# Attention with forget gates, then a gated feed-forward: mask and decay become rows of the score contraction, q and k reach their tiles through a staging tile and a second transfer

## The chip, the cores and the metric

The kernel runs on one core of a Trainium2 chip. The core has a matrix engine (TensorE, PE in the profile, with its weight loads as PEld), a vector engine (VectorE, DVE), an activation engine (ScalarE, ACT), a general engine (GpSimd, POOL) and a queue processor (SyncE, SP) that issues nearly all DMAs here. Each engine executes its own list of instructions strictly in order, and the engines wait for each other on semaphores. The metric is the time of one execution on the device in microseconds (us), the median of several runs.

## The reference

There are 8 batches with 8 heads each, sequences of 576 positions and 64 numbers per head. Attention has a causal mask and a decay that accumulates from a forget gate `f`. A feed-forward layer follows, with a convolution of three taps along the sequence that gates its hidden layer.

```python
scores = q @ k.T / sqrt(64)
cum    = cumsum(log(clip(f, 1e-4, 1)))
scores = where(key > query, -1e9, scores + cum[query] - cum[key])
x      = softmax(scores) @ v                 # heads side by side: [8, 576, 512]
h      = relu(x @ w_in)                      # [8, 576, 1024]
conv   = w[0]*h[s-1] + w[1]*h[s] + w[2]*h[s+1]
out    = (h * sigmoid(conv)) @ w_out         # [8, 576, 512]
```

## The kernel before

**Groups.** Attention works in 16 groups of four heads, numbered `hb` 0 to 15; two groups make one batch `b`. For each group the scores are computed with keys on the partitions and queries along the free axis, in 128-wide blocks, and only where the key block is not wholly in the future. The blocks on the diagonal (`sd`, two steps per group, line 342), the blocks below it (`so`, four steps, line 364) and the 64-wide tail block (`st`, line 322) are separate steps, each filling a PSUM tile of 1024 columns, and each is followed by an exponential on ACT (`ed`, `eo`, `et`). The product with v follows (`pv`), its normalisation on DVE (`n`, `m`), a turn to the layout of the feed-forward (`t`, `tx`), and then per batch eight steps of the first feed-forward product (`f`, line 425), of the rectifier on ACT (`r`), the convolution on DVE (`c`, `d`), the gate's function on ACT (`a`), the gating on DVE (`g`), and the second product (`o`, line 469), its copy out of PSUM (`e`) and its store (`s`).

**q and k.** A group's q and k stand in one of four tiles `qk` (`RING` = 4, so that group `hb` reuses the tile of group `hb - 4`, and its steps wait for the scores of that group, the list `old` in the code). q and k are 32-bit numbers in memory. For groups 2 to 15 a transposing DMA (`q{hb}.0` for q, `q{hb}.1` for k, line 180) reads them as pairs of 16-bit halves and writes 128 partitions of 2304 columns: the odd partitions hold the upper halves, which are the numbers in bf16, and the even partitions hold the lower halves, which are not wanted. All 128 partitions go into the contraction, so the even ones must be overwritten, with zeros but for three partitions that carry the decay: `cum` in bf16 on the side of q against -1 on the side of k, and two bf16 pieces of `cum` on the side of k against 1 on the side of q. For groups 2 to 7 this is done by DVE (`cl`, line 186, one instruction per side over 128x2304) and two small DMAs from a copy of the rows in memory (`rw`, lines 202 and 203). For groups 8 to 15 it is done by DMAs alone (`fi`, lines 194 and 196): zeros from a tensor `blank` in memory and four rows (the fourth of zeros) from `image`. Groups 0 and 1 are loaded plainly and turned by TensorE (`tp`, `cl`), since they are needed at once; in group 0 the decay is added by two further matmuls per score matmul (lines 315 and 317).

**The causal mask.** In groups 0 to 7 (`MASK_PE`) a matmul ahead of each half of a diagonal step, and ahead of the tail step, writes -1e30 above the diagonal (line 320), and the scores accumulate on it. In groups 8 to 15 the exponential writes to a 32-bit tile, and POOL selects from it with an affine condition (`md`, `mt`, lines 356 and 335).

**What sets the order.** A list written out by hand (`ORDER`) names every step once. The program walks through it and appends each step's instructions to its engine's list, so the order of the names decides the order on every engine, SP's queue included; a step that has a choice of engines carries it after an `@`. Buffers go round in the order of the list. SP waits in place: a DMA whose semaphore has not arrived holds back all DMAs behind it. Every DMA also waits for the landing of the eighth before it, since eight semaphores go round.

## Time and profile before

| | |
|---|---|
| runs | 246.43, 249.28, 249.78 us; median 249.28 us |
| span of the profiled execution, from its first to its last instruction | 244.1 us |
| median of the runs less that span (launch and end lie around it) | 5.2 us |
| busy share of the span: PE, DVE, ACT, POOL | 93%, 84%, 85%, 22% |
| share of the chain that ended last on PE | 78% |
| DMA | 49.68 MB in 120176 packets, mean 204 GB/s |

A line of the profile names the engine, the line of the program, the operation, and out<-in by the names of the tiles (without buffer numbers), with shapes as partitions x elements. `SPq` is SP's queue; the duration there is the time that the issue of the DMA took, not the transfer. "Landing" is the time from the issue until the last of the transfer's semaphore updates.

### The profile page before, as it was taken

How to read it: one execution, taken by the hardware profiler on the slowest of the kernel's cores; microseconds unless marked ns; L12 is line 12 of the kernel's file. 1: busy time of each engine (PE TensorE's matmuls, PEld its weight loads, DVE VectorE, ACT ScalarE, POOL GpSimd, SP SyncE). 2: the span in 40 equal slices, each digit the busy share in tenths (PEclk: the TensorE clock that was granted, in tenths of full speed). 3: DMA queues.
4: the chain of work that ended last, by engine and by line, in shares of the span. 5: the costliest groups of instructions: out<-in, count | busy, mean ns of one | idle time of the engine just before them, and what ended most of it. 6: DMA issues, size and time to landing. Idle time of an engine off the chain costs nothing.

```text
span 244.1 us, 6385 instructions
## 1 busy us (share of the span) xinstructions
PE 226.9 (93%) x2627; PEld 145.0 (59%) x2627; DVE 205.1 (84%) x323; ACT 206.9 (85%) x278; POOL 52.9 (22%) x77
## 2 busy tenths in 40 slices
PE   0899899779999999999999999999999999999991
PEld 0787585547556676575557755675666566444440
DVE  5735359999998999999999889996998889999931
ACT  2868677999998999999999999999988995798442
POOL 8020520205220020030402570245311311000000
PEclk9999999999999999999999999999999999999999
DMA  6999999999999999999999999969999950641326
GB/s 192 328 159 243 304 204 192 202 253 279 204 188 205 228 158 240 229 314 186 198 256 246 187 209 257 273 134 222 194 260 188 236 140 3 168 157 62 142 86 216
DMA packets 120176, 49.68 MB, mean 204 GB/s; under 512 B 109759, under 2 KB 110271, under 8 KB 120147
## 3 DMA queue, kind: packets, MB, share of 16 engines
q1 hardware_dynamic: 119981, 48.97, 92.4%
q8 instruction: 20, 0.33, 0.6%
q10 hardware_dynamic: 166, 0.31, 0.4%
q14 instruction: 9, 0.07, 0.1%
HBM read 21.11 MB, written 10.17 MB: 128 GB/s over the span
## 4 chain that ended last, share of the span: by engine, by line
PE 78%; DVE 7%; DMA 6%; ACT 4%; issue 1%; ACTq 1%; SPq 1%; DVEq 0%
PE ps L474 24%; PE ps L429 20%; PE ps L312 15%; PE ps L389 7%; DMA qk<-in_q_dram 3%; PE ps L320 3%; PE ps L394 3%; PE ps L166 2%; PE ps L414 2%; DVE u L446 2%; ACT pp L370 2%; DMA pd<-in_moe_conv_w_dram 2%; DVE u L448 2%; DVE qk L186 1%; DMA qk<-image 1%
## 5 line engine op out<-in xcount | busy, mean ns | idle before, releaser
L429 PE MATMUL ps<-xt,w_in_f 128*128 128x512 f16 (+1 forms) x512 | 69.9, 286 | 0.0
L370 ACT ACTIVATE pp<-ps 128x1024 f16<-128x1024 f32 x64 | 64.7, 1032 | 4.2 <-PE ps L312 2.7
L474 PE MATMUL ps<-w_out_f,hg 128*128 128x512 f16 x288 | 66.8, 379 | 0.0
L312 PE MATMUL ps<-qk 128*128 128x128 bf16 (+2 forms) x576 | 63.4, 240 | 1.6 <-ACT pp L353 0.8
L446 DVE SCALAR_TENSOR_TENSOR u<-ht,cwt 128x576 f32<-128x576 f16 x64 | 52.7, 837 | 3.6 <-ACT ht L440 3.4
L451 ACT ACTIVATE hg<-u,cw 128x576 f16<-128x576 f32 x64 | 48.7, 782 | 5.9 <-DVE u L448 5.8
L448 DVE SCALAR_TENSOR_TENSOR u<-ht,cwt,u 128x576 f32<-128x576 f16 x64 | 53.2, 846 | 0.5
L429 PEld LDWEIGHTS <-w_in_f 128*128 128x128 f16 x512 | 34.3, 98 | 28.5
L312 PEld LDWEIGHTS <-qk 128*128 128x128 bf16 x576 | 39.2, 98 | 19.8 <-issue 3.3
L440 ACT ACTIVATE ht<-ps 128x576 f16<-128x576 f32 x64 | 41.0, 663 | 6.0 <-DVE hg L458 2.7
L474 PEld LDWEIGHTS <-hg 128*128 128x128 f16 x288 | 26.9, 98 | 28.8
L458 DVE SCALAR_TENSOR_TENSOR hg<-hg,ht 128x576 f16<-128x576 f16 x51 | 38.7, 771 | 0.6 <-ACT hg L451 0.5
L356 POOL TENSOR_SCALAR_AFFINE_SELECT pp<-pd 128x1024 f16<-128x1024 f32 x16 | 19.7, 1244 | 53.6 <-ACT pd L353 53.6
L389 PE MATMUL ps<-va,pp 128*128 128x65 f16 x640 | 24.8, 193 | 1.1 <-DVE va L217 1.0
L389 PEld LDWEIGHTS <-pp 128*128 128x128 f16 x640 | 22.6, 97 | 3.7 <-DVE va L217 1.3
L405 DVE TENSOR_TENSOR xm<-ps,rc 128x896 f16<-128x896 f32 (+1 forms) x32 | 23.9, 751 | 0.5
L353 ACT ACTIVATE pp<-ps 128x1024 f16<-128x1024 f32 x16 | 16.6, 1039 | 4.7 <-PE ps L312 3.9
L353 ACT ACTIVATE pd<-ps 128x1024 f32<-128x1024 f32 x16 | 16.2, 1023 | 1.2 <-PE ps L312 1.0
L217 POOL CAST va<-vf 128x1024 f16<-128x1024 f32 x8 | 10.0, 1252 | 32.1 <-DMA vf<-in_v_dram 27.8
L320 PE MATMUL ps<-mask,ident 128*128 128x512 bf16 (+1 forms) x40 | 14.3, 359 | 1.5 <-ACT pp L370 0.8
L403 DVE RECIPROCAL rc<-ps 128x14 f32<-128x14 f32 (+1 forms) x32 | 6.7, 208 | 8.6 <-PE ps L394 5.5
L479 ACT COPY ob<-ps 128x1024 f32<-128x1024 f32 (+1 forms) x14 | 12.9, 919 | 0.3 <-issue 0.2
(83 smaller groups left out, 176.4 us busy)
## 6 DMA issues: line engine op xcount, KB each, us to landing
vf<-in_v_dram SPq DMA_DIRECT2D x32, 256.0 KB, 7.7
out_dram<-ob SPq DMA_DIRECT2D x14, 512.0 KB, 3.7
qk<-blank SPq DMA_DIRECT2D x8, 540.0 KB, 6.2
ob<-in_moe_w_in_dram SPq DMA_DIRECT2D x4, 512.0 KB, 6.3
ob<-in_moe_w_out_dram SPq DMA_DIRECT2D x4, 512.0 KB
out_dram<-ob SPq DMA_DIRECT2D x6, 256.0 KB, 7.2
vf<-in_v_dram SPq DMA_DIRECT2D x8, 128.0 KB, 5.9
hg<-in_q_dram SPq DMA_DIRECT2D x2, 288.0 KB
```

The lines of the kernel that those rows point to most:

```text
L312: nc.tensor.matmul(o, tk[:, h * S + k0:h * S + k0 + 128], tq[:, h * S + q0:h * S + q0 + n], start=first, stop=last and not by_matmul(hb, h))
L353: nc.scalar.activation(o, ps_of(f"sd{i}").rearrange("p (s c) -> p s c", s=2), AF.Exp, scale=SCALE)
L370: nc.scalar.activation(pair(i)[:, s, 512:1536], ps_of(f"so{i}.{s}"), AF.Exp, scale=SCALE)
L389: nc.tensor.matmul(ps[:, c:c + D + 1], block(hb, h, m, n), va[:, h, m, 0:D + 1], start=(m == 0), stop=(m == n))
L405: nc.vector.tensor_tensor(xm[:, CUT * D * u:CUT * D * u + nj * k * D].rearrange("p (j x d) -> p j x d", x=k, d=D), got[:, :, :, 0:D], r.un ...
L429: nc.tensor.matmul(ps[:, t0:t1], w_in_f16[:, cc, 128 * ff:128 * (ff + 1)], xt[:, cc // 2, x:x + t1 - t0], start=(cc == 0), stop=(cc == NCC ...
L440: nc.scalar.activation(ht_of(b, ff)[:, 2:2 + S], ps_of(f"f{b}.{ff}")[:, 0:S], AF.Relu, scale=1.0 if (b, ff) in LATE else 0.5)
L446: nc.vector.scalar_tensor_tensor(u, ht[:, 1:1 + S], cwt[:, ff, 0:1], ht[:, 2:2 + S], op0=ALU.mult, op1=ALU.add)
L448: nc.vector.scalar_tensor_tensor(u, ht[:, 3:3 + S], cwt[:, ff, 1:2], u, op0=ALU.mult, op1=ALU.add)
L451: nc.scalar.activation(hg_of(b, ff), u_t[slot[f"c{b}.{ff}", "u"]], AF.Sigmoid if (b, ff) in LATE else AF.Tanh, scale=cw[:, ff, 1:2])
L458: nc.vector.scalar_tensor_tensor(hv, hv, 1.0, ht_of(b, ff)[:, 2:2 + S], op0=ALU.add, op1=ALU.mult)
L474: nc.tensor.matmul(ps[:, 512 * (c % 2):512 * (c % 2 + 1)], w, w_out_f16[:, ff, :], start=(ff == 0), stop=(ff == NFF - 1))
```

## The change

**Mask and decay as rows.** Below the 64 numbers of a head, the contraction gets further rows: four for the decay (partitions 64 to 67, two pieces of `cum` on either side) and 43 for the causal mask (68 to 110). Ordinary blocks contract over 68 rows (`ROWS`), blocks on the diagonal over 111 (`EDGE`). The mask rows hold powers of a small step on the side of q and large negative numbers on the side of k, so that a sum over the rows is near zero at and below the diagonal and hugely negative above it; each row covers three columns. POOL makes the pattern `edge` once, with one memset and eleven affine selections of 128x128, and it is then copied into partitions 64 to 127 of the four `qk` tiles, both sides (`px{t}.{side}`, eight steps of two copies over 64x2048 and 64x256): tile 0 on DVE, tiles 1 to 3 on POOL. The copies stay valid for the whole run, apart from the decay rows, which `rw` overwrites for each group. The mask matmuls, POOL's selections, DVE's `cl` of groups 2 to 7, and the tensor `blank` with its fills go away.

**Staging and a second transfer.** For groups 2 to 15 the transposing DMA now writes one of two staging tiles `sg` (`NSG` = 2), and a second DMA (`cp{hb}.{side}`, 64 partitions of 2304 bf16, 288 KB) copies its odd partitions to partitions 0 to 63 of the `qk` tile. The transposing load waits for a free `sg` tile, which means for the landing of the `cp` that read it last; `cp` waits for the landing of its load and for the scores of group `hb - 4`. `rw` is now two DMAs of two rows each for every group, and waits for the `px` steps of its tile.

**Order.** The list is the old one with the new steps put in, and the loads moved back behind the `cp` that frees their staging tile where two tiles would not do. In SP's queue around groups 8 and 9 the old program has the following (`qk1` is the tile of group 9, `qk0` that of group 8; `vf0` is the v of batch 4, `ob` are stores):

```order
L180 DMA_TRANSPOSE qk1_86<-in_k_dram 128x2304
L180 DMA_TRANSPOSE qk0_85<-in_k_dram 128x2304
L180 DMA_TRANSPOSE qk1_86<-in_q_dram 128x2304
L180 DMA_TRANSPOSE qk0_85<-in_q_dram 128x2304
L194 DMA qk1_86<-blank_66 60x4x1152
L196 DMA qk1_86<-image_65 4x2x2304
L194 DMA qk0_85<-blank_66 60x4x1152
L196 DMA qk0_85<-image_65 4x2x2304
L209 DMA vf0_89<-in_v_dram 128x8x64
```

The new program has at the same place (lines 171, 178 and 189/190 are the load, `cp` and `rw`):

```order
L171 DMA_TRANSPOSE sg0_86<-in_k_dram 128x2304
L171 DMA_TRANSPOSE sg1_87<-in_k_dram 128x2304
L178 DMA qk1_83<-sg0_86 64x2304
L171 DMA_TRANSPOSE sg0_86<-in_q_dram 128x2304
L178 DMA qk1_83<-sg0_86 64x2304
L171 DMA_TRANSPOSE sg0_86<-in_q_dram 128x2304
L189 DMA qk1_83<-image_65 2x2304
L190 DMA qk1_83<-image_65 2x2304
L178 DMA qk0_82<-sg0_86 64x2304
L178 DMA qk0_82<-sg1_87 64x2304
L189 DMA qk0_82<-image_65 2x2304
L190 DMA qk0_82<-image_65 2x2304
```

Four loads that stood in a row are now the first two in a row, and then copy, load, copy, load, and two copies, all through the tile `sg0` but for the last.

On POOL, after the memsets at the start, the old program casts v and the weights of the feed-forward as they land (`va1` is the v of group 1, without which `pv1.0` can't start):

```order
L217 CAST va0_91<-vf0_89 128x4x4x64
L219 CAST va0_91<-vf0_89 64x4x64
L518 CAST w_in_f16_69<-ob0_125 128x2x512
L217 CAST va1_92<-vf0_89 128x4x4x64
L518 CAST w_in_f16_69<-ob1_126 128x2x512
```

The new one has the copies of the pattern ahead of them (lines 183 and 185; 204 and 206 are the casts of v, 471 that of the weights; each pair of rows stands for one `px` step, and the next three pairs, for `qk2` and `qk3`, are left out at the dots):

```order
L204 CAST va0_90<-vf0_88 128x4x4x64
L206 CAST va0_90<-vf0_88 64x4x64
L183 COPY qk1_83<-edge_74 64x4x512
L185 COPY qk1_83<-edge_74 64x4x64
L183 COPY qk1_83<-edge_74 64x4x512
L185 COPY qk1_83<-edge_74 64x4x64
...
L183 COPY qk3_85<-edge_74 64x4x512
L185 COPY qk3_85<-edge_74 64x4x64
L471 CAST w_in_f16_68<-ob0_121 128x2x512
L204 CAST va1_91<-vf0_88 128x4x4x64
```

Twelve copies now stand between the cast for group 0 and the cast for group 1.

The diff, without the lines of the list but for its head, and without those declarations that only go away:

```diff
 ORDER = """
-dca cw ld0 ld1 ld0.0.0 tp0.0.0 dcl ...
+dca cw px0.0@DVE px0.1@DVE ld0 ld1 ld0.0.0 tp0.0.0 dcl ...
 """
...
+    NSG = 2
-    NCL = 8
-    MASK_PE = (0, 1, 2, 3, 4, 5, 6, 7,)
+    ROWS, EDGE = 68, 111
+    STEP, FAR = 2.0 ** -55, -2.0 ** 16
...
+    sg_t = [cpool.tile([128, HS], BF16, name=f"sg{t}") for t in range(NSG)]
...
     def turn_qk(hb, p, side):
-            nc.tensor.transpose(o[:, 128 * j:128 * (j + 1)], i[:, 128 * j:128 * (j + 1)], ident_b)
+            nc.tensor.transpose(o[0:64, 128 * j:128 * (j + 1)], i[:, 128 * j + 1:128 * (j + 1):2], ident_b)
...
-    def load_qk(hb, h0, nh, side):
+    def load_qk(hb, side):
+        src = (q, k)[side]
         nc.sync.dma_start_transpose(
-            t.bitcast(U16)[:, h0 * S:(h0 + nh) * S],
+            sg_t[slot[f"q{hb}.{side}", "sg"]].bitcast(U16),
...
-    def clamp(hb, h0, nh, side):
-    def fill(hb):
...
+    def pack(hb, side):
+        t = sg_t[slot[f"q{hb}.{side}", "sg"]]
+        odd = bass.AP(tensor=t.tensor, offset=int(t.offset) + HS, ap=[[2 * HS, 64], [1, HS]])
+        nc.sync.dma_start(qk_t[hb % RING][0:64, HS * side:HS * (side + 1)], odd)
+
+    def edge_rows(t, side, e):
+        copy = {"ACT": nc.scalar.copy, "POOL": nc.gpsimd.tensor_copy, "DVE": nc.vector.tensor_copy}[e]
+        o = qk_t[t][64:128, HS * side:HS * (side + 1)].rearrange("p (h s) -> p h s", h=HH)
+        copy(o[:, :, 0:512].rearrange("p h (m j) -> p h m j", j=128),
+             edge[64:128, side].unsqueeze(1).unsqueeze(1).broadcast_to((64, HH, 4, 128)))
+        copy(o[:, :, 512:S], edge[64:128, side, 0:SL].unsqueeze(1).broadcast_to((64, HH, SL)))
 
     def rows_of(hb):
+        c, t = slice(hb * HH, (hb + 1) * HH), qk_t[hb % RING]
+        nc.sync.dma_start(t[64:66, 0:HS], image[:, c, :].rearrange("j h s -> j (h s)"))
+        nc.sync.dma_start(t[66:68, HS:2 * HS], image[:, c, :].rearrange("j h s -> j (h s)"))
...
-    def scores(o, hb, h, k0, q0, n, m=128, first=True, last=True):
+    def scores(o, hb, h, k0, q0, n, m=128, rows=ROWS):
         tq, tk = stq_t[hb % RING], stk_t[hb % RING]
-        nc.tensor.matmul(o, tk[:, h * S + k0:h * S + k0 + 128], tq[:, h * S + q0:h * S + q0 + n],
-                         start=first, stop=last and not by_matmul(hb, h))
+        nc.tensor.matmul(o, tk[0:rows, h * S + k0:h * S + k0 + m], tq[0:rows, h * S + q0:h * S + q0 + n],
+                         start=True, stop=not by_matmul(hb, h))
...
-    def masked(o, n, j):
-    def tail_mask(hb):
-    def diag_mask(i):
...
             for side in range(2):
-                add(f"q{hb}.{side}", "SP", old, lambda hb=hb, side=side: load_qk(hb, 0, 4, side))
+                add(f"q{hb}.{side}", "SP", [], lambda hb=hb, side=side: load_qk(hb, side), take=["sg"])
+                add(f"cp{hb}.{side}", "SP", [f"q{hb}.{side}"] + old, lambda hb=hb, side=side: pack(hb, side),
+                    give=[("sg", f"q{hb}.{side}")])
+            add(f"rw{hb}", "SP", ["ki"] + old + px, lambda hb=hb: rows_of(hb))
+            ready = [[f"rw{hb}", f"cp{hb}.0", f"cp{hb}.1"]] * 2
+        ready = [r + px for r in ready]
```

More of the change, by code (lines that the diff above doesn't have):

```diff
@@ L277, in decay_image @@
     def decay_image(e):
-        for j, a, h in ((0, 0, 0), (1, 1, 0), (2, 1, 1)):
-            {"SP": nc.sync, "POOL": nc.gpsimd}[e].dma_start(image[j, a], kc[BH * h:BH * (h + 1)])
-    def constants():
-        nc.sync.dma_start(image[1:3, 0].rearrange("j h s -> h j s"), plus.unsqueeze(1).broadcast_to((BH, 2, S)))
-        nc.sync.dma_start(image[0, 1], minus)
-        nc.sync.dma_start(image[3].rearrange("a h s -> h a s"), zero.rearrange("h (a s) -> h a s", a=2))
-        nc.sync.dma_start(blank, zero[0:60])
-    def warm_up(name):
-        for x in range(2):
-            nc.tensor.matmul(ps_of(name)[:, 512 * x:512 * (x + 1)], quiet[:, 0:128], quiet, start=True, stop=True)
+        for j in range(2):
+            {"SP": nc.sync, "POOL": nc.gpsimd}[e].dma_start(image[j], kc[BH * j:BH * (j + 1)])
     def conv_weights():
@@ L521 @@
     add("cwt", "DVE", ["cw"], conv_ratios, give=[("ps", "cw")])
-    for x in range(0):
-        add(f"wu{x}", "PE", [], lambda x=x: warm_up(f"wu{x}"), take=["ps"])
-        add(f"wd{x}", "PE", [], lambda: None, behind=[f"wu{x}"], give=[("ps", f"wu{x}")])
-    add("zc", "SP", [], constants)
     add("dca", "DVE", [], lambda: nc.vector.tensor_scalar(fsb, fsb, 1e-4, 1.0, op0=ALU.max, op1=ALU.min))
@@ L534 @@
             add(f"{w}c{j}", "POOL/ACT/DVE", [f"{w}{j}"], lambda e, w=w, j=j: stage_cast(w, j, e), give=[("ob", f"{w}{j}")])
+    for t in range(RING):
+        for side in range(2):
+            add(f"px{t}.{side}", "POOL/DVE/ACT", [], lambda e, t=t, side=side: edge_rows(t, side, e))
     for hb in range(NHB):
@@ L538 @@
         was = hb - RING
+        px = [f"px{hb % RING}.{side}" for side in range(2)]
         old = [f"st{was}"] + [f"sd{2 * was + y}" for y in range(2)] + [
```

149 lines of the change are left out of this document (43 added, 106 removed).

## The prediction

> **What bounds the kernel now.** I read the page's busy shares first, then its chain, then a table by stages, and last SP's queue.
>
> ```profile
> span 244.1 us, 6385 instructions
> PE 226.9 (93%) x2627; PEld 145.0 (59%) x2627; DVE 205.1 (84%) x323; ACT 206.9 (85%) x278; POOL 52.9 (22%) x77
> PE   0899899779999999999999999999999999999991
> PE 78%; DVE 7%; DMA 6%; ACT 4%; issue 1%; ACTq 1%; SPq 1%; DVEq 0%
> 40.00:60.00 20.00, 16.67 (x247) 11.51 (x246) 19.79 (x30) 19.47 (x28) 4.29 (x4) 1.00 1.11 242
> 107.00:133.00 26.00, 26.00 (x272) 15.82 (x270) 24.66 (x36) 25.48 (x36) 6.06 (x6) 1.00 1.17 231
> ```
>
> The chain runs on PE. Of the 40 slices of 6.1 us in the third row, each from the tenth to the last but one is 90% busy or more, and from 107 to 133 us PE has no gap (the columns of the last rows are the stretch, its length, then PE, PEld, DVE, ACT and POOL busy, the granted clock, the DMA share and GB/s). From 40 to 60 PE lacks 3.3 us, with DVE and ACT full. So a matmul taken away after 60 us is worth its time, as long as its inputs come. The last figures of each row warn of that: the DMA engines have work all the time. How q and k arrive stands in SP's queue; this is the turn for groups 8 and 9:
>
> ```profile
> 84.94 0.61 SPq L203 DMA_DIRECT2D qk<-image  x1
> 85.65 6.12 SPq L180 DMA_TRANSPOSE qk<-in_k_dram  x2
> 91.82 5.02 SPq L180 DMA_TRANSPOSE qk<-in_q_dram  x2
> 96.95 0.95 SPq L194 DMA_DIRECT2D qk<-blank  x1
> ...
> 100.64 0.41 SPq L209 DMA_DIRECT2D vf<-in_v_dram  x1
> 101.11 0.57 SPq L495 DMA_DIRECT2D out_dram<-ob  x1
> ...
> 102.40 2.96 SPq L495 DMA_DIRECT2D out_dram<-ob  x1
> 105.40 2.06 SPq L209 DMA_DIRECT2D vf<-in_v_dram  x2
> 107.56 4.86 SPq L180 DMA_TRANSPOSE qk<-in_q_dram  x1
> 106.54 1.03 ACT L353 ACTIVATE pd<-ps 128x1024 f32<-128x1024 f32 x1
> PE ps L312 <- DMA qk<-image: 0.4, 1, 0.4
> ```
>
> Four loads go out back to back in 11.1 us, the fills follow, then v and stores, and 21.9 us after the first load the next turn starts. The first exponential of group 9 begins 20.9 us after its first load was issued: PE's matmuls wait for q and k only 0.4 us in the whole run (last line), but there is little to spare.
>
> **What goes away.** PE loses 40 mask matmuls, and their price is the distance to the next matmul, not the listed duration:
>
> ```profile
> L320 PE MATMUL ps<-mask,ident 128*128 128x512 bf16 (+1 forms) x40 | 14.3, 359 | 1.5 <-ACT pp L370 0.8
> 43.65 0.38 PE L320 MATMUL ps<-mask,ident 128*128 128x512 bf16 x1
> 43.87 0.38 PE L312 MATMUL ps<-qk 128*128 128x128 bf16 x4
> L356 POOL TENSOR_SCALAR_AFFINE_SELECT pp<-pd 128x1024 f16<-128x1024 f32 x16 | 19.7, 1244 | 53.6 <-ACT pd L353 53.6
> L186 DVE TENSOR_SCALAR qk<-qk,lim 128x2304 uint16<-128x2304 uint16 x12 | 10.3, 874 | 2.3 <-DMA qk<-in_q_dram 2.3
> ```
>
> That is 0.22 us for 32 of them and about half for the 8 short ones, 7.9 us in all. Groups 4 to 7 fall after 58 us, where PE is full: 3.9 us are certain if inputs come in time. Groups 0 to 3 lie where ACT, DVE and DMA share the chain, so their 3.9 may stay hidden. POOL's 19.7 us of selections were beside other work (the chain has no POOL), and of DVE's 10.3 us some is on the chain before 60 us, but there the transfers are late next. Fewer contraction rows I cost at nothing: the columns streamed stay the same, and no row here shows a score matmul with fewer rows, so I bound it by none to the masks' size either way.
>
> **What POOL adds.** Six `px` steps stand between the casts for groups 0 and 1.
>
> ```profile
> 26.68 1.04 POOL L217 CAST va<-vf 128x1024 f16<-128x1024 f32 x1
> 32.22 1.16 PE L389 MATMUL ps<-va,pp 128*128 128x65 f16 x32
> 17.51 0.39 POOL L219 CAST va<-vf 64x256 f16<-64x256 f32 x1
> ```
>
> POOL's cast takes 1.04 us for 1024 elements and 0.39 for 256; a `px` step of 2048 and 256 elements is thus about 2.5 us, between 1.3 (if bf16 copies go twice as fast) and 3.2 us. POOL is free from 17.9; six steps end at 32.9, then a weight cast, then `va1.0` at 35. `pv1.0`, which ran at 32.22, waits 2 to 3 us on PE, and everything behind it on PE too. Tile 0's copies on DVE stand ahead of the decay's sum; at the 874 ns that DVE took for 2304 columns they cost some 2 us, which the turning of group 0 hides up to 11.8 us; at half that rate group 0 starts 2 us later.
>
> **What SP adds.** The chain load, landing, `cp`, landing, next load replaces loads back to back. Its prices:
>
> ```profile
> DMA to landing us min/median/max: 4.8/6.2/6.4
> image<-kc SPq DMA_DIRECT2D x3, 72.0 KB, 3.4
> out_dram<-ob SPq DMA_DIRECT2D x14, 512.0 KB, 3.7
> qk<-blank SPq DMA_DIRECT2D x8, 540.0 KB, 6.2
> ```
>
> A load (the first row; it is that of the transfers into `qk`) lands 4.8 to 6.4 us after issue; the chain leaves less ahead of it in the queue, so I take 4.8. `cp`, from SBUF, 288 KB, has no row; 72 KB out of SBUF took 3.4, 512 KB 3.7, a fill of 540 KB behind loads 6.2. I take 3.5, with 3.3 and 6.2 as ends. The Trainium skill ("DMA: Bandwidth & Descriptors", "Anatomy of one DMA — SWDGE (gpsimd) path") fits a fixed 2.0 us plus bytes over 436 GB/s: an estimate of 2.7 for `cp`, by which each of some nine `cp`s in series would be 0.8 shorter and the sum below 7 us less. For the two rows from SBUF the fit gives 2.2 and 3.2, where this trace has 3.4 and 3.7.
>
> Groups 8/9, from the first load: landed 4.8; `cp9.1` landed 8.3; `q9.0` 13.1; `cp9.0` 16.6; `q8.0` 21.4; two `cp` issues (0.95 as the fill's) and two row DMAs (0.61) take 3.1: 24.5; v and stores as now, 100.64 to 107.56, 6.9: 31.4. Now it is 21.9, so 9.5 us are lost.
>
> ```profile
> 125.88 0.41 SPq L209 DMA_DIRECT2D vf<-in_v_dram  x1
> 127.08 6.17 SPq L209 DMA_DIRECT2D vf<-in_v_dram  x3
> 133.35 6.78 SPq L180 DMA_TRANSPOSE qk<-in_q_dram  x2
> 156.83 1.02 ACT L353 ACTIVATE pd<-ps 128x1024 f32<-128x1024 f32 x1
> 22.24 0.30 SPq L202 DMA_DIRECT2D qk<-image  x1
> 26.00 5.64 SPq L180 DMA_TRANSPOSE qk<-in_q_dram  x1
> 37.90 2.00 SPq L209 DMA_DIRECT2D vf<-in_v_dram  x3
> 40.00 0.39 SPq L202 DMA_DIRECT2D qk<-image  x1
> 63.77 3.96 SPq L180 DMA_TRANSPOSE qk<-in_q_dram  x1
> ```
>
> Groups 10/11 start with two loads (3.1 apart, half of 6.12): 7.9, then 11.4, 16.2, 19.7, 24.5, issues 27.6, v and stores 125.88 to 133.35, 7.5: 35.1 against 25.8 now, 9.3 lost. Group 12: 4.8, 8.3, 13.1, `cp13.0` behind that load about 14.5, `q12.1` 19.3, `cp12.1` 22.8, against 23.0 now from 133.35 to the scores ahead of the exponential at 156.83: nothing more.
>
> Before group 9: `rw1` waits for POOL to 23 instead of 22.24. `q3.0`, issued at 26.00, waits for the landing of `cp2.0`, issued at 24.9 behind the weights: 28.4. Two loads and three v: 36.6; `cp3.0` landed 40.1, `q4.1` 44.9, `rw3` 45.9 instead of 40.00. One more round trip beside the weights' loads to 63.77 loses some 2, groups 6/7 (4.8, 8.3, 13.1, 14.5, 19.3, issues and v 4.6: 23.9 against 21.9 from 63.77 to 85.65) another 2: about 10 in all.
>
> Sum: 10 + 9.5 + 9.3 = 28.8. Against it, the store of 2.96 us and the v of 2.06 and 6.17 were long because the queue was full (neighbours take 0.4 to 0.6); a chain that lets the DMA engines idle gives some 3 us back in each of three such blocks, 9. Remaining: 20 us by the time group 12 starts, PE having nothing else to do in its order. The 88 us from there to the end stay as they are (groups 14 and 15 come no later than that), and the masks' 3.9 and POOL's 2 to 3 vanish in the waits. So the span is 244.1 + 20 = 264, and with the 5.2 us between span and median 269 us.
>
> Ends: in series stand three loads in each of the turns from group 8 to 12 and some four before, 13, and nine `cp`s. If a load lands 1 us sooner in a shorter queue (`cp` at 3.3 adds 2), 15 us go: 254. Load and `cp` both at 6.2 add 13 x 1.4 and 9 x 2.7, 42 us: 311.
>
> **Rivals.**
>
> *The queue keeps pace.* If the landings were so short that a turn fits into PE's 25.8 us, PE would remain the bound. Groups 8/9 need three loads and two `cp`s in series, plus 10 us of issues: it decides at 15.8 us for the five, such as 3.4 for each load and 2.8 for each `cp`. For it speaks that these landings were measured in a full queue; against it, that the smallest row of a load is 4.8. Then POOL's 2.3 stay and the masks' 3.9 to 7.9 go: 243.7 to 247.7. Chance 0.13, with 0.05 of it below 244.3.
>
> *Only the beginning is late.* The waits on `old` at a load are gone, so SP may run ahead and catch up after group 5; then POOL's 2 to 3 and `rw3`'s 6 remain, less the masks of groups 4 to 7: 252 to 256, two fifths of it still within 2%. Chance 0.13.
>
> *Congested landings.* The upper ends in half of the links or more: 285 to 311. For it speaks that v and stores still precede the loads in the queue. Chance 0.11.
>
> *Half clock after waits.* The trace shows matmuls at half rate after the 7 us in which PE waited at the start:
>
> ```profile
> 8.15 3.73 PE ps L166 x36
> 15.07 0.50 PE ps L166 x9
> ```
>
> 0.104 us each, then 0.056: 1.7 us lost in one such stretch. The forecast has five waits of several us; all but the last are followed by another wait that swallows the loss, but if each counts, 8.5 us: 278. The Trainium skill ("TensorE: Matmul & The Clock Gate", "Part 1: The HAM clock gate") says that an idle window of about 3.4 us halves the clock; the trace agrees at the start, and after 11 us no wait is long enough to show it. Chance 0.08.
>
> **The numbers.** My forecast, lateness of 7 to 36 us, has 0.55. Runs of before spread by 1.3% and about 2% can be told from no change: faster means under 244.3, slower over 254.3. Faster 0.05, from the first rival; same 0.13, its other 0.08 and 0.05 of the second; slower 0.82. The range leaves out the first rival and the upper half of the congested case, 0.19: 251 to 292 us.
>
> **What would show it.** In the changed profile: successive turns of loads for groups 8/9, 10/11 and 12/13 some 28 to 32 us apart where now 22 and 26; PE's waits listed on DMA `qk<-sg` or `qk<-image`, several us each, at groups 3, 9, 8, 11 and 12; DMA share clearly under 1 between 60 and 170 us; a POOL `px` copy near 2.1 us. Wrong would be: `cp` landing in under 3 us and PE without gaps after 60 us, then the first rival holds; or SP waiting on PE at `cp`, then the queue was ahead.

## The result, and the profile after

The changed kernel takes 321.2 us (median of 4 runs, 320.5 to 323.6), the kernel before 248.1 us on the same chip: a ratio of 1.296, 95% interval 1.287 to 1.305. The direction was forecast, the size was not: 269 us were predicted, with a range of 251 to 292. In five of the variants below (short copies alone, four tiles with short copies, the beginning alone, both with 24 extra copies) one or two of the four runs, the profiled one among them, came out over 1.5% above the fastest and are left out of the ratio, though not of the median given in us.

These are lines of the changed kernel's page: span, busy times, three rows of the 40 slices (8 us each here), the first DMA queue (packets, MB, share of the time of 16 DMA engines) and the chain by engine.

```profile
span 318.8 us, 6332 instructions
PE 249.7 (78%) x2587; PEld 159.4 (50%) x2587; DVE 195.7 (61%) x305; ACT 208.0 (65%) x278; POOL 46.0 (14%) x74
PE   1997592585879549863799759993999969999993
PEclk9998598596879958995599975998699998999998
DMA  8999787969995699938994599758979999136315
q1 hardware_dynamic: 119640, 52.11, 82.6%
DMA 38%; PE 33%; SPq 17%; ACT 4%; issue 3%; DVE 2%; POOL 2%; ACTq 0%; POOLq 0%
```

Before, the chain had 78% PE and 6% DMA; now DMA and SP's queue hold 55% of it. PE is below 90% in 20 of the 40 slices, and its clock falls to 5 and 6 tenths behind the holes. The row of the queue matters most, because the prediction never used it. The same row of the kernel before reads:

```profile
q1 hardware_dynamic: 119981, 48.97, 92.4%
```

The share is the sum of the packets' times over 16 engines: 92.4% of 244.1 us, 226 us, before; now 82.6% of 318.8, 263 us. It is no exact measure of work done, since packets that are on their way together are counted each, so that it goes over 1 where transfers crowd (1.07 on average from 20 to 195 us before), and a packet that is held up counts longer. Two things happened at once: the packets take 37 us more, and what is left of the span grew from 19 to 55 us. Before, the 19 us lay at the end: in the last 49 us the share is 0.40. Now it is 0.90 from 20 to 260 us. The waits show who stands still. First the two rows of PE's waits for q, k and their rows, then SP's own queue, where L171 is the transposing load and `qk<-sg` the packing copy:

```profile
PE ps L288 <- DMA qk<-image: 41.7, 9, 9.6
PE ps L288 <- DMA qk<-sg: 6.7, 2, 4.1
SPq L171 <- DMA qk<-sg: 54.7, 14, 7.8
```

Fourteen loads stood for 54.7 us until a copy had landed and its staging tile was free. The turn for groups 8 and 9, in SP's queue of the changed kernel (start, duration, what is issued; L178 is the copy, L189 and L190 the rows):

```profile
120.40 7.32 SPq L171 DMA_TRANSPOSE sg<-in_k_dram  x2
127.89 0.49 SPq L178 DMA_DIRECT2D qk<-sg  x1
132.47 1.96 SPq L171 DMA_TRANSPOSE sg<-in_q_dram  x1
138.11 0.47 SPq L178 DMA_DIRECT2D qk<-sg  x1
142.28 1.95 SPq L171 DMA_TRANSPOSE sg<-in_q_dram  x1
144.28 0.42 SPq L189 DMA_DIRECT2D qk<-image  x1
144.76 0.25 SPq L190 DMA_DIRECT2D qk<-image  x1
146.43 1.12 SPq L178 DMA_DIRECT2D qk<-sg  x2
147.59 0.45 SPq L189 DMA_DIRECT2D qk<-image  x1
...
148.52 0.41 SPq L196 DMA_DIRECT2D vf<-in_v_dram  x1
...
155.60 7.49 SPq L171 DMA_TRANSPOSE sg<-in_q_dram  x2
```

The turn lasts 35.2 us; it was 21.9, and 31.4 were predicted. The next starts at 155.60 instead of 107.56, so 48.0 us late, and the end is 74.7 us late.

The trace also gives the time of each DMA packet. These are the packets of 4608 bytes, which but for some 60 are the rows of the packing copies (number, median and 95th percentile in ns, their sum over 16 engines), and the sum of all packets:

```
kernel     4608-byte packets   median   95%    sum/16    all packets, sum/16
before           85             305     371     1.5 us        228.3 us
after          1852             478     721    51.1 us        266.6 us
```

A copy is 64 such packets, so 28 copies take about 50 us of all 16 engines, 1.8 us each. What went away, the fills of 2304-byte packets, freed 17.5 us (26.2 to 8.7).

### The profile page after: what moved, and what is told of

The parts are those of the page before. It is cut to its first block, busy times and chain, and to the rows that moved or that the text cites. A ratio compares the mean times of both kernels' runs of the same rounds, so it can differ in the third digit from the quotient of the medians.

```text
span 318.8 us, 6332 instructions
## 1 busy us (share of the span) xinstructions
PE 249.7 (78%) x2587; PEld 159.4 (50%) x2587; DVE 195.7 (61%) x305; ACT 208.0 (65%) x278; POOL 46.0 (14%) x74
## 3 DMA queue, kind: packets, MB, share of 16 engines
q1 hardware_dynamic: 119640, 52.11, 82.6%
## 4 chain that ended last, share of the span: by engine, by line
DMA 38%; PE 33%; SPq 17%; ACT 4%; issue 3%; DVE 2%; POOL 2%; ACTq 0%; POOLq 0%
DMA qk<-sg 20%; PE ps L427 12%; SPq L171 9%; PE ps L288 8%; PE ps L382 8%; DMA qk<-image 6%; DMA sg<-in_q_dram 5%; DMA sg<-in_k_dram 3%; SPq L196 3%; DMA vf<-in_v_dram 3%; PE ps L342 2%; DMA u<-in_f_dram 2%; SPq L189 2%; PE ps L367 1%; SPq L448 1%
## 5 line engine op out<-in xcount | busy, mean ns | idle before, releaser
L288 PE MATMUL ps<-qk 111*128 111x128 bf16 (+3 forms) x576 | 73.1, 270 | 55.9 <-DMA qk<-image 41.7
L288 PEld LDWEIGHTS <-qk 68*128 68x128 bf16 (+2 forms) x576 | 44.0, 112 | 76.9 <-issue 36.1
L382 PE MATMUL ps<-xt,w_in_f 128*128 128x512 f16 (+1 forms) x512 | 73.7, 295 | 0.1
L313 ACT ACTIVATE pp<-ps 128x1024 f16<-128x1024 f32 x32 | 32.6, 1023 | 62.8 <-PE ps L288 61.5
L427 PE MATMUL ps<-w_out_f,hg 128*128 128x512 f16 x288 | 71.2, 397 | 0.0
L323 ACT ACTIVATE pp<-ps 128x1024 f16<-128x1024 f32 x64 | 64.6, 1025 | 9.4 <-PE ps L288 7.2
L427 PEld LDWEIGHTS <-hg 128*128 128x128 f16 x288 | 27.9, 101 | 31.7 <-issue 4.4
L342 PE MATMUL ps<-va,pp 128*128 128x65 f16 x640 | 29.3, 207 | 0.8 <-ACT ht L393 0.8
L342 PEld LDWEIGHTS <-pp 128*128 128x128 f16 x640 | 27.5, 108 | 4.1 <-issue 1.2
L358 DVE TENSOR_TENSOR xm<-ps,rc 128x896 f16<-128x896 f32 (+1 forms) x32 | 23.9, 753 | 0.5
L206 POOL CAST va<-vf 64x256 f16<-64x256 f32 x6 | 5.2, 860 | 103.7 <-PE ps L288 58.9
L370 DVE COPY xt<-ps 128x1152 f16<-128x1152 f16 x9 | 6.8, 757 | 10.9 <-PE ps L367 7.9
L183 POOL COPY qk<-edge 64x2048 bf16<-64x2048 bf16 x6 | 11.4, 1908 | 0.0
```

The source lines that it names most:

```text
L288: nc.tensor.matmul(o, tk[0:rows, h * S + k0:h * S + k0 + m], tq[0:rows, h * S + q0:h * S + q0 + n], start=True, stop=not by_matmul(hb, h))
L313: nc.scalar.activation(pair(i)[:, :, 0:512], ps_of(f"sd{i}").rearrange("p (s c) -> p s c", s=2), AF.Exp, scale=SCALE)
L323: nc.scalar.activation(pair(i)[:, s, 512:1536], ps_of(f"so{i}.{s}"), AF.Exp, scale=SCALE)
L342: nc.tensor.matmul(ps[:, c:c + D + 1], block(hb, h, m, n), va[:, h, m, 0:D + 1], start=(m == 0), stop=(m == n))
L382: nc.tensor.matmul(ps[:, t0:t1], w_in_f16[:, cc, 128 * ff:128 * (ff + 1)], xt[:, cc // 2, x:x + t1 - t0], start=(cc == 0), stop=(cc == NCC ...
L427: nc.tensor.matmul(ps[:, 512 * (c % 2):512 * (c % 2 + 1)], w, w_out_f16[:, ff, :], start=(ff == 0), stop=(ff == NFF - 1))
```

## The experiments

The first theory was the prediction's own, sharpened by the wait of 54.7 us: **the serial chain**, load, copy, load, through two staging tiles in a queue that issues in order. Its rivals were the **bytes** of the copies, the **beginning** (late casts on POOL, copies behind the weights), and the **half clock** of PE.

**Four staging tiles, loads at their old places.**

```diff
-    NSG = 2
+    NSG = 4
-    RING, NP, NPT, NVA, ..., NOB = 4, 6, 4, 4, ..., 4
+    RING, NP, NPT, NVA, ..., NOB = 4, 6, 3, 3, ..., 3
-... q9.1 t5 a1.7 tx5@DVE q8.1 so12.1 ... cp9.1 q9.0 cp9.0 q8.0 rw9 sd15 ...
+... q9.1 t5 a1.7 tx5@DVE q8.1 q9.0 so12.1 ... q8.0 f2.0 cp9.0 cp9.1 rw9 sd15 ...
```

> The changed kernel with four staging tiles instead of two and with the loads of q and k, the packing copies and the row transfers at the places that loads, clamps and fills had before the change (all loads of a turn back to back, copies behind them). To make room there are three tiles of v's casts, of output stages and of tail probabilities instead of four. Theory (serial chain: a load cannot be issued before the copy that frees its staging tile has landed, and the queue of SP stands still meanwhile): the four loads of a turn go out within about 12 us again, PE's waits on q and k fall from about 60 us to under 15, the mean clock comes back to at least 0.97 from 0.868, and the time is 250 to 262 us. Rival 1 (the copies' bytes: 28 copies of 288 KB more on DMA engines that were full already): the bytes are the same, so the time stays above 300 us. Rival 2 (the late casts of POOL at the start, and the half clock that follows): the start is the same, so at least the first 30 us of lateness up to group 5 stay, 280 us or more.

Measured: 289.2 us, ratio 1.166 (1.158 to 1.174). The chain theory alone falls: no load waits for a copy any more, yet only 32 of 73 us come back. The bytes alone, which were to keep the time above 300 us, fall too; the 280 us or more of a late beginning are not contradicted. The same turn in SP's queue, the four loads, and the DMA row and queue of that run:

```profile
112.51 10.35 SPq L171 DMA_TRANSPOSE sg<-in_k_dram  x2
122.90 4.49 SPq L171 DMA_TRANSPOSE sg<-in_q_dram  x2
DMA  7998299999999999999999999999999995072315
q1 hardware_dynamic: 119640, 52.11, 96.0%
```

The loads go out back to back, but issuing them takes 14.8 us where it took 11.1, with the engines now at 90% or more in all slices but two from the second to the 33rd: 96.0% of 289.0 us is 277 us of packet time. That looks like a bound of its own; the runs with short copies test it.

**Four staging tiles, the changed order kept.** The edit is the first two pairs of lines above.

> The changed kernel with four staging tiles (and the same three smaller pools as in the run before), but the changed kernel's order of loads and copies is kept. A load then no longer waits for the copy ahead of it to land; but SP still stands at each copy until the load of that copy has landed. Theory (serial chain): of each link of about 5 us for a load and 4.2 to 5.6 us for a copy the second half goes, so about half of the 73 us comes back: 275 to 292 us, and the turn of groups 8 and 9, 35.2 us now, is 26 to 30 us. Rival 1 (bytes): above 300 us. Rival 3 (only the waiting for a free tile matters, not SP's standing at the copies): as with the old order, 250 to 262 us.

Measured: 295.4 us, ratio 1.194 (1.187 to 1.200), a little above what the chain theory gave. The turn of groups 8 and 9 takes 31.4 us, where 26 to 30 were expected. Freeing the loads from the copies brings 26 us, putting them back to back another 6. In both runs the engines are full most of the time (94.6% here), so the two are not to be read as the full worth of each half.

**Copies of an eighth of the columns, all else as changed.**

```diff
-        ... ap=[[2 * HS, 64], [1, HS]])
-        nc.sync.dma_start(qk_t[hb % RING][0:64, HS * side:HS * (side + 1)], odd)
+        n = HS if hb < RING else HS // 8
+        ... ap=[[2 * HS, 64], [1, n]])
+        nc.sync.dma_start(qk_t[hb % RING][0:64, HS * side:HS * side + n], odd)
```

> The changed kernel with its two staging tiles and its order, but from group 4 on each packing copy moves only the first 288 of the 2304 columns; the rest of the scores is made from the columns of earlier groups. Waits and queue are as before, the bytes of 24 copies fall from 6.9 MB to 0.9 MB. Theory (serial chain, in which a copy's landing is a fixed part and its bytes, 288 KB at about 150 GB/s being 1.9 us): each copy lands 1.7 us sooner, about 2.5 instead of 4.2; with about 11 copies in series from group 4 to 13 the time falls by 15 to 25 us to 296 to 306 us. Rival 1 (bytes): 6.0 of 52.8 MB are gone, so about 36 us: 280 to 287 us.

Measured: 277.2 us, ratio 1.115 (1.107 to 1.124): 44 us less with the chain left as it was, even more than the bytes' number. The packets of 4608 bytes fell from 51.1 to 7.7 us of engine time. SP's waits of loads for a copy fell from 54.7 to 30.9 us. So the bytes count, through the engines' time and through each copy's landing; this run does not divide the two.

**Both at once.**

> Both edits at once: four staging tiles with the old places of the loads, and packing copies of 288 of 2304 columns from group 4 on (the rest of the scores is made from columns of earlier groups). Apart they gave 289 and 277 us, where the whole change takes 321. Theory (two causes that add: the copies' time on the 16 DMA engines, 2.3 us of each copy, and the serial chain through two tiles that leaves the engines idle): from group 5 on the kernel runs at the pace of before, 175 us from the first exponential of group 5 to the end, which starts at about 88 to 90 us as in both single runs: 260 to 270 us with the 5 us around the span. Rival (either alone is enough, since the longer of the two sets the pace): 274 to 280 us, as with short copies alone.

Measured: 262.3 us, ratio 1.054 (1.046 to 1.063), where the theory of two adding causes had put it. From the first exponential of group 5, at 84.4 us, the kernel runs nearly at the pace of before (180.1 us to the end, against 175.4); most of what is left, 15.7 us, lies ahead of it.

**The bytes in the kernel before.** 24 extra copies, for whose data no engine waits:

```diff
+    spare = cpool.tile([64, 2304], BF16, name="spare")
+    for x in range(24):
+        add(f"xx{x}", "SP", [], lambda: nc.sync.dma_start(spare,
+            w_in_f16.rearrange("p c f -> p (c f)")[0:64, 0:2304].bitcast(BF16)))
```

> The kernel before the change with 24 extra copies of 288 KB from SBUF to a spare tile of 64 partitions (0 to 63, 4608 bytes each), spread over SP's transfers of groups 4 to 14. No instruction of another engine waits for them; three tiles of v's casts, output stages and tail probabilities instead of four make the room. This is the price of the copies' bytes alone, without chain, staging or mask rows. Theory (bytes: each copy holds the 16 DMA engines for 2.0 to 2.3 us, and these were busy for 228 of 244 us): 276 to 283 us of engine time, so 265 to 285 us. Rival (only the chain and the waits of SP cost): 248 to 254 us.

Measured: 283.0 us, ratio 1.134 (1.123 to 1.145). No staging and no mask rows, and 34 us are lost, nearly as much as the change loses with four tiles (41). But the run is not free of a chain: all 24 copies write the one tile `spare`, and SP stood at ten of them until the copy before had landed. SP's wait in this run and, below it, in the next one, with 128 partitions:

```profile
SPq L527 <- DMA spare<-w_in_f: 18.0, 10, 3.9
SPq L527 <- DMA spare<-w_in_f: 9.9, 8, 3.3
```

So the 34 us are the price of the bytes and of this standing together, and how much each of them has is not shown. PE and DMA of this run, in slices of 7.1 us:

```profile
PE   0998798797699869859995899579899499999992
DMA  7999999999999799899999999999999792073315
```

DMA is at 90% or more in all but two slices from the second to the 31st, and PE is below 90% in 17 of the first 32. The three smaller pools are part of the 34 us; the run without a full copy below has them too, and loses 9 us in all.

**The same bytes to 128 partitions**, `spare` being 128 x 1152 and the source 128 partitions too:

> As the run with 24 extra copies to 64 partitions, at the same places and with the same 288 KB each, but to 128 partitions of 2304 bytes. In the changed kernel a packet of 4608 bytes to partitions 0 to 63 takes 478 ns in the median where the first ones of a lone copy take 180, and packets of 2304 bytes to partitions spread over all 128 take 93 to 111 ns. Theory (the writes of partitions 0 to 63 share half of the ways into SBUF and hold the engines up): packets of about 100 ns, 24 copies cost 20 us of engine time instead of 50, 250 to 262 us. Rival (the bytes cost the same wherever they land): the same time as with 64 partitions.

Measured: 267.1 us, ratio 1.070 (1.060 to 1.081), 5 us above the range given but 16 us below the run with 64; 8 us less of SP's standing may be part of that. The packets:

```
extra copies          packets        median     sum/16    per copy
to partitions 0-63    24 x 64,4608 B  362 ns    34.3 us    1.43 us
to all 128            24 x 128,2304 B 100 ns    22.9 us    0.95 us
```

The sums are those of the size class less what the kernel before has in it (1.5 and 26.2 us). So a copy confined to 64 partitions takes half as much engine time again as the same bytes over 128. The Trainium skill ("SBUF — State Buffer", "Door 1: The DMA port swizzle (why `[64,N]` ≈ `[32,N]`)") says that partitions 0 to 63 reach only 8 of SBUF's 16 DMA ports and gives 196 GB/s for them, at 1 MiB, against 328 over all 128. The runs agree in direction: 1.43 to 0.95 is a factor of 1.5, the page's figures make 1.7. Source, destination and the packets' length changed together here, so which of them does it stays open.

**The beginning alone.**

```diff
-... px1.1@POOL px2.0@POOL px2.1@POOL px3.0@POOL px3.1@POOL cwt ...
+... px1.1@POOL cwt ...
-... st1 wi0 so2.0 sd3 wi2 wic0@POOL wi3 et1 eo2.0 cp2.0 cp2.1 rw2 n0.0 ... wic2@POOL ...
+... st1 px2.0@DVE px2.1@DVE cp2.0 cp2.1 rw2 wi0 so2.0 sd3 wi2 wic0@POOL wi3 et1 eo2.0 n0.0 ... wic2@POOL px3.0@POOL px3.1@POOL ...
```

> The changed kernel with only its beginning altered: the two packing copies and the rows of group 2 are issued ahead of three of the weights' transfers (1.5 MB) instead of behind them, the mask rows of ring tile 2 are copied by DVE, and those of tile 3 by POOL behind the casts of the weights. Theory (the first 15 us of lateness come from there: the copy of group 2 landed at 35 us behind the weights, and the loads of group 3 wait for it): the first exponential of group 3 comes at 48 to 53 us instead of 60.1, and the whole takes 308 to 314 us. Rival (the later chain catches the gain, since it sets its own pace from the loads of group 4 on): 318 to 322 us.

Measured: 320.3 us, ratio 1.280 (1.265 to 1.294): nearer to the rival. By the ratio it is some 318 us, 3 to 4 less than the changed kernel, with intervals that overlap. In the profiled run group 2's first exponential comes at 31.7 instead of 36.8 us, group 3's at 57.3 instead of 60.1, and by group 5 (90.4 and 91.0) nothing is left of it. There, time won ahead of the chain is lost in it.

**PE kept busy in its waits.**

```diff
+    WARM = {"sd5": 14, "sd6": 36, "sd9": 13, "sd10": 11, "sd13": 30, ...}
+    def warm(name):
+        for _ in range(WARM.get(name, 0)):
+            nc.tensor.matmul(ps_of(name)[:, 0:512], ident_b, ident_b.unsqueeze(1).broadcast_to((128, 4, 128)), ...)
     def diag_scores(i):
         ps = ps_of(f"sd{i}")
+        warm(f"sd{i}")
```

> The changed kernel with 183 extra matmuls of 512 columns on constant tiles, put on TensorE ahead of the eleven score steps at which it waited 2.2 to 9.6 us for q, k or their rows (52 us in all); they fill about four fifths of each wait (0.22 us each, 40 us in all), so that the clock is not cut. Their results are overwritten. Theory (half clock after the waits is on the path: PE was busy for 249.7 us with 40 matmuls fewer than before's 226.9): the mean granted clock comes back over 0.95 and the time falls by 10 to 20 us to 300 to 312 us. Rival (the chain of loads and copies sets its own pace and swallows what PE loses): clock back, time within 316 to 326 us.

Measured: 321.9 us, ratio 1.303 (1.293 to 1.313), with the mean clock at 0.944 instead of 0.868. Two stretches of the changed kernel, and below them the same two of this run (stretch, length, busy time of PE, PEld, DVE, ACT, POOL, granted clock, DMA share, GB/s):

```profile
50.00:60.00 10.00, 0.96 (x10) 0.99 (x11) 2.95 (x4) 1.04 (x2) 0.00 (x0) 0.70 1.14 170
120.00:155.00 35.00, 23.41 (x259) 16.08 (x256) 22.46 (x33) 20.67 (x29) 2.05 (x2) 0.79 0.88 138
```

```profile
50.00:60.00 10.00, 6.65 (x33) 2.91 (x31) 2.18 (x3) 0.27 (x1) 0.00 (x0) 0.97 1.01 158
120.00:155.00 35.00, 29.90 (x295) 17.36 (x293) 22.03 (x33) 20.00 (x29) 2.39 (x2) 0.95 0.81 133
```

The clock is back and the time is not. The extra matmuls did not swallow the gain themselves: behind them PE still waited 20.9 us for the rows of q and k, and the first exponentials of groups 9 and 12 come when they did (148.3 and 224.8 us, against 148.2 and 224.3). So the slow clock is a mark that the waits leave, not a cause of the 73 us.

**The complete change with order and beginning repaired**: four tiles, loads at their old places, and the beginning as above.

> The changed kernel, complete, with four staging tiles and the old places of the loads (289 us so far), and with the beginning altered as in the run of the beginning alone: the copies and rows of group 2 ahead of the last three transfers of w_in, the mask rows of ring tile 3 behind the casts. Theory (the copies' bytes bound it: 277 us of engine time in the run with four tiles, 96% of its span): 282 to 288 us, little gained. Rival (the 17 us of lateness at group 5 come from the beginning, and are independent of the rest): 270 to 276 us.

Measured: 281.8 us, ratio 1.138 (1.129 to 1.146), just under what the theory gave. In the run with four tiles one weight transfer had stood for a cast (three issues took 9.9 us instead of 1.4, as there were fewer output stages); that is gone here too. Its DMA row and queue:

```profile
DMA  7999999999999999999999999999999995073415
q1 hardware_dynamic: 119640, 52.11, 98.2%
```

From 20 to 228 us the share is 1.13 on average, more than the 1.07 of before, and DMA and SP's queue hold 60% of the chain. So the transfers set the pace of this kernel up to there. That no better order exists is not shown; but even in the changed kernel itself, where the engines stood idle more, the same packets took 266.6 us.

**All three edits together**, with short copies from group 4 on:

> As the run with four staging tiles and copies of 288 columns from group 4 on (262 us), with the beginning altered in the same way as well (the rest of the scores of groups 4 to 15 is again made from columns of earlier groups). What is then left of the change are the full copies of groups 2 and 3, the short ones, the mask rows and the missing mask matmuls. Theory (the 14 us that were still lost lie in the order at the beginning): 248 to 256 us. Rival (they lie in the full copies of groups 2 and 3 themselves, beside the weights' transfers): 258 to 264 us.

Measured: 257.3 us, ratio 1.040 (1.032 to 1.048), between the two. Here short copies are worth 24.5 us (281.8 to 257.3): same order, same number of transfers, no load that waits for a copy, and only the bytes differ. It is the cleanest price of them that these runs give.

**No full copy left.**

```diff
-        n = HS if hb < RING else HS // 8
+        n = HS // 8
+    for t in (2, 3):
+        add(f"zi{t}", "DVE", [], lambda t=t: nc.vector.memset(qk_t[t][0:64, 0:2 * HS], 0.0))
```

> As the last run (four staging tiles, old places of the loads, altered beginning; 257 us), but the packing copies of groups 2 and 3 are cut to 288 columns as well, so that no full copy is left; ring tiles 2 and 3 are zeroed on DVE behind the decay's sum, about 2 us in all. That run was still 9 us late at group 3. Theory (the four full copies of groups 2 and 3 are the rest, 2.3 us of the engines each and landing behind the weights): 249 to 253 us. Rival (what remains is the second transfer as such: a copy and its rows can only be issued when the load has landed, whatever its size): 255 to 259 us.

Measured: 255.3 us, ratio 1.037 (1.030 to 1.043), within the rival's range. The zeroing took 4.0 us on DVE, not 2, and made group 1 start at 31.0 us instead of 27.0; group 3 still came earlier than in the run before (51.3 against 54.6). Against the 1.040 of the run before, the gain is 1 us and within the noise; the four full copies may be worth some 4 us more, which the zeroing would have taken back. How the last 9 us divide between the second transfer as such, the smaller pools, the mask rows and the zeroing is not settled.

**The masks alone**, left out of the kernel before:

```diff
     def tail_scores(hb):
-        on = hb in MASK_PE
+        on = False
     def diag_scores(i):
-        ps, on = ps_of(f"sd{i}"), i // 2 in MASK_PE
+        ps, on = ps_of(f"sd{i}"), False
-        ... AF.Exp, scale=SCALE)
+        ... AF.Exp, scale=SCALE * 1e-6)
```

> The kernel before the change, with its 40 mask matmuls left out and nothing put in their place; the exponentials of the diagonal and tail blocks get a scale a million times smaller so that the unmasked scores stay finite (the same instructions, other values). This is the change's gain alone. By the prediction: 0.22 us for each of 32 matmuls and half of it for 8, so 7.9 us at most and 3.9 us from groups 4 to 7: 240 to 244.5 us against 248. If the masks were hidden by ACT, DVE and DMA everywhere: 247 to 249 us. If the other engines (DVE at 84%, ACT at 85%) take over as the bound after group 4: 245 to 247 us.

Measured: 246.6 us against 248.0, ratio 0.996 (0.994 to 0.999). By the ratio the 40 matmuls are worth 0.9 us, 0.2 to 1.6. Where PE had no gap before (first two rows), it has some now (last two):

```profile
60.00:85.00 25.00, 25.00 (x273) 15.31 (x271) 23.43 (x34) 23.47 (x34) 3.93 (x3) 1.00 1.04 205
85.00:107.00 22.00, 21.99 (x292) 14.73 (x291) 21.74 (x35) 21.30 (x30) 1.59 (x2) 1.00 1.08 223
60.00:85.00 25.00, 22.75 (x250) 13.74 (x248) 23.53 (x31) 23.16 (x33) 4.75 (x4) 1.00 1.06 200
85.00:107.00 22.00, 20.60 (x257) 13.42 (x256) 21.84 (x36) 20.54 (x30) 1.90 (x2) 1.00 1.07 214
```

PE does 3.6 us less in these 47 us, and groups 5 to 8 start at the same times as before, within 1.0 us (68.3, 85.1, 92.2, 108.5 instead of 68.7, 84.8, 92.0, 107.5). So other work takes over: DVE is busy for 21.84 of the 22 us from 85 to 107, and the chain that ended last, which ran almost wholly on PE between 60 and 107 us before, now runs through DVE for stretches of it and, from 64 to 70.8 us, through one transfer of weights (5.4 us) and its cast on POOL. The expectation had named this case, DVE or ACT as the next bound, at 245 to 247 us. The mask matmuls, which the change was to save on PE, are thus worth 0.4%. What the fills, DVE's `cl` and POOL's selections cost, which the change removes too, was not measured alone.

Side by side, with the time of all DMA packets over 16 engines in the profiled run:

```
kernel                                   us     ratio    DMA packets   span
before                                 248.1     1          228.3      244.1
after                                  321.2    1.296       266.6      318.8
four tiles, changed order              295.4    1.194       282.0      294.8
four tiles, old places                 289.2    1.166       280.4      289.0
  and beginning altered                281.8    1.138       276.3      278.0
    and copies an eighth               257.3    1.040       220.1      258.4
      and all copies an eighth         255.3    1.037       208.9      253.0
copies an eighth alone                 277.2    1.115       217.8      279.2
before with 24 copies, 64 partitions   283.0    1.134       267.3      283.0
before with 24 copies, 128 partitions  267.1    1.070       249.7      265.8
```

## Why the prediction was wrong

By one path of this table the 73 us are 39 us of order (two tiles, alternation, beginning), 25 us of the copies' bytes, and 9 us that stay. Taken the other way round, the short copies alone give 44 and tiles, order and beginning after them 20: the two causes overlap, since short copies also shorten the links of the chain. The forecast had 29 us for order, less 9 given back, and nothing for the bytes. Now the steps:

**What bounds the kernel.** "The chain runs on PE" was read as one bound. There were more beside it: the packets at 92.4% of the span, 1.07 on average from 20 to 195 us, and DVE at 21.74 of the 22 us from 85 to 107. The prediction did say that "the DMA engines have work all the time", but only as a warning. The masks' "3.9 us are certain" fell with it: a PE that is full does not mean that PE alone sets the end, and 0.9 us is what came.

**The copies' cost, the step that failed.** The sum priced a copy by its landing (3.5 us) and its issue (0.95), and had no term for the time that it takes of the 16 engines. That term is 50 us, and 38 in the sum of all packets with what went away, on engines that had 19 us to spare, nearly all behind 195 us. What it is worth in the end, the runs with short copies show: 24.5 us with order and beginning repaired (281.8 to 257.3), 44 with the chain in place. The page gave a warning, not the size: net of the fills the queue carries 3.1 MB more (48.97 to 52.11), which at the page's average of 48.97 MB in 226 us is an estimate of 14 us. What no row of before showed is that the copies' packets would take 478 ns each.

**"Given back", 9 us.** The same omission with the sign turned round. The block of v and stores in the turn of 8 and 9 was to shrink by 3 us in an idler queue; it took 7.1 us (148.52 to 155.60) where 6.9 were quoted.

**The chain.** Its mechanism was right, as the 54.7 us of SP's waits and the runs with four tiles show, and its links were too short by a little. For groups 8 and 9: first load 7.5 us for 4.8, because two loads are issued together and the first copy waits behind both; copies 4.6 and 4.2 for 3.5; loads 5.6 and 4.2 for 4.8; copies and rows at the end 2.1 for 3.1; v and stores 7.1 for 6.9. That is 35.2 for 31.4, and 3 more for what was not given back. The signs that the prediction named for this part came: turns 35.2 and 36.6 us apart (28 to 32 were named), a DMA share of 0.91 from 60 to 170 us, and waits of PE at groups 3, 9, 8, 11 and 12, among others. By the fit that the prediction took from the Trainium skill ("DMA: Bandwidth & Descriptors", "Anatomy of one DMA — SWDGE (gpsimd) path") a copy would land in 2.7 us. The section is about transfers that GpSimd issues, and these go out from SP. The trace has 4.2 for one with no other load, store or copy beside it (issued at 165.32, and the load that waits for it at 169.49), so the measurement decides against the fit here.

**Before group 9, 10 us.** It was 34.8: `q9.1` went out at 120.40 instead of 85.65. By `rw3` (53.82 for 40.00) it was 13.8, of which 5.9 had been forecast; `q3.0` went out at 35.01, where 28.4 was worked out, because the copy of group 2 landed behind 1.5 MB of weights. The price of that transfer was not taken from the queue in front of it. Groups 6 and 7 then took 33.0 us for 23.9: the same chain as later, which the prediction here replaced by a shorter one. The run of the beginning alone shows that this early part does not simply add: of its 5 us at group 2, 0.6 are left at group 5.

**After group 12, nothing.** From `q12.0` to the end it took 126.6 us (192.17 to 318.8) instead of 110.8: the turn of 12 and 13 is a chain like the others, and it needed 28 us to its last rows (220.33), not 22.8.

**The 5.2 us from span to median.** They are not launch and end: the profiled run of before took 246.43 us itself, 2.3 over its span of 244.1. The rest of the 5.2 is that it was the fastest of the three runs. Of the miss of 52 us this is a small part.

**What held.** A `px` step took 2.33 us for 2.5, and POOL's lateness left no trace in the end: when its cast for group 1 was done, at 33.3 us, PE was waiting for the copy of group 2, until 35.75. Fewer contraction rows cost nothing and win nothing there, as the widest score matmul of the kernel before and of a run with an undisturbed clock (both short copies and four tiles, from 160 to 215 us) suggest; the columns are rows x columns, type, count, busy time and mean ns:

```profile
L312 PE MATMUL ps<-qk 128*128 128x448 bf16 x64 | 22.6, 353 | 0.0
```

```profile
L289 PE MATMUL ps<-qk 68*128 68x448 bf16 x18 | 6.3, 351 | 0.0
```

**The rivals.** "Congested landings", 285 to 311 us with a chance of 0.11, came nearest, but as a price of the links, not as a bound. "Half clock after waits" happens: the rule that an idle window of about 3.4 us halves the clock (the Trainium skill, "TensorE: Matmul & The Clock Gate", "Part 1: The HAM clock gate") fits the stretches above: in the trace of the changed kernel the granted clock goes to half from 54.00 to 64.24 us, when PE has stood since about 49.5, and to half ten times more, for 3.41 us or a multiple of it each time but the last. But it is worth nothing here, as the run with the waits filled shows. The range ended at 292 because its upper end, too, was made from landings alone.

## What to carry to other kernels

Before costing a transfer by its latency, read the share of the 16 DMA engines in the queue's row, see in which stretches it is full, and add the new packets to it as one adds matmuls to PE: here a kernel at 92%, with its idle time at the end, had little room for a second pass over its inputs, and the best order tried still lost 34 us. A staging buffer that is filled and emptied by the same in-order queue makes the queue wait for itself when it has fewer tiles than a turn has transfers: four tiles for two were worth 26 us. And before paying for a removal, leave the removed work out alone and time that: here the 40 mask matmuls were worth 0.4%.

## What was not expected of the hardware

A packing copy that has the engines to itself slows down in its second half. These are some of the 64 packets of the copy issued at 165.32 us in the changed kernel, each 4608 bytes, in order of their start:

```
number   start us   ns
   1     166.454   179
  32     166.789   179
  33     166.809   295
  47     166.947   649
  53     167.135   702
  64     167.601   487
```

The first 32 take about 180 ns, the others 295 to 722; 295 KB in 1.63 us are 180 GB/s. Packets of 256 bytes, those of the loads above all, grew as well beside such copies, from 154.5 us of engine time in the kernel before to 166.5 with four tiles at the old places and 178.6 in the changed order, for the same 107136 packets. So a copy can cost more than its own packets; in the run with 24 extra copies to 64 partitions, though, the 256-byte packets took only 157.6 us.

And what one edit is worth depends on what else is repaired: short copies brought 44 us with the chain in place and 24.5 with order and beginning repaired. The altered beginning brought 7 us with four tiles (289.2 to 281.8), and by the ratios 3 to 4 both with short copies besides (1.054 to 1.040) and with the chain in place, where the intervals overlap.
